# Turns of u and of the scores at the start of a fused attention and gated feed-forward kernel: their places in the transpose queue are given by a table

## The chip, the cores and the metric

One core of one Trainium2 chip. The metric is the device time of one execution in microseconds (us); less is better. The engines are called by the names of the profile: PE (TensorE, matrix products), DVE (VectorE), ACT (ScalarE), POOL (GpSimd) and SP (SyncE). SP computes nothing here: it issues all DMA transposes, one after another. POOL issues nearly all loads from memory, and ACT issues the stores.

## The reference

Eight sequences of 3008 tokens pass through a gated attention with squared-ReLU scores, and the result through a feed-forward layer with activation h cos(h):

```
scores = (z @ z.T) / S                  # z: 8 x 3008 x 64, S = 3008
attn   = max(scores, 0) ** 2
x      = u * (attn @ v)                 # u, v: 8 x 3008 x 256
h      = x @ w_in                       # w_in: 256 x 2048
out    = (h * cos(h)) @ w_out           # w_out: 2048 x 256
```

Since the same z stands on both sides, the matrix of scores is symmetric. Inputs and output are in float32; the kernel computes in float16 and accumulates in float32.

## The kernel before, in words

A sequence (the code calls it a batch, b = 0 to 7) is cut into six columns c of 512 tokens, and the scores into square tiles (c, R) of column and row, 512 by 512. The columns pass one after another. For each tile PE makes the scores (`s_matmuls`, L265), ACT or DVE takes the ReLU (L301, L299), and DVE squares it (L303) into one of 18 slots of SBUF, named `s`. PE then multiplies the tiles of a column with v into two banks of PSUM, `acc` (L353, or L466 for columns that use a scheme with seven products in place of eight, whose sums DVE prepares at L423, L425 and L435). At a column's end `finish` gates: DVE multiplies `acc` with the transposed u, named `ut`, into x (L382). That frees the two banks for the next column. The feed-forward layer follows 512 tokens at a time: `h_quantum` (PE L500, ACT L504, DVE L507) and `y_quantum` (PE L517), spread between the work of the attention.

Because of the symmetry a tile (c, R) with R > c serves column c as it is, and column R when it is transposed. The transpose is a DMA from slot to slot, issued by SP (L310). Columns 0 to 2 of the first batch are different: `direct` says that all six of their tiles are computed, so that they wait for no transpose. Their tiles with R = 3, 4 and 5 are turned all the same, since columns 3, 4 and 5 read them: nine transposes, called (0,3) to (2,5) in this text. Pairs (3,4), (3,5) and (4,5) follow, and from then on the kernel is in its steady course. Column 3 reads (0,3), (1,3) and (2,3), in the sums at L423.

Other transposes share SP's queue: `turn_u` (L181) makes `ut` of one column, called ut(0) to ut(5) here; `turn_z` (L144) and the tiles on the diagonal (L290) have theirs. `load_u`, `load_v`, `load_w_in` and `load_w_out` (all at L121) are issued by POOL. u is staged in two buffers `ust` in turn, so that u of column c + 2 is loaded after u of column c has been turned. `hold` lets a load or a turn of u or z wait for the PE product that was written down last before it, so that it isn't issued too early. A score transpose has no such hold: it waits for its data and its slot.

What sets the order: the kernel writes its steps into a list `events`, each with a time in units in which a column takes eight (U = 8) and a rank, sorts the list and calls the steps in that order. The framework then schedules what was recorded, engine by engine, by priority and by what is ready; `chain` holds PE to the written order, and `after(..., NOSYNC)` holds one instruction behind another without a wait on the chip. In this kernel a score transpose is recorded in `s_squares`, right behind the last square of its tile, and `turn_u` of the first batch stands at times 1, 5 and 10 for columns 0, 1 and 2:

```python
at(t + c * U + (1 if b or c not in (1, 2) else -3 * c), 0, lambda b=b, c=c: turn_u(b, c))
```

`use` notes from when to when each slot is needed, and `place` gives out the slots by it.

Of the kernel before, what the change touches and what calls it, by code (L numbers as in the profile page):

```python
# [14 lines left out]
def kernel(  # L15
# [9 lines left out]
    nc = tc.nc  # L25
# [21 lines left out]
    U = 8  # L47
# [186 lines left out]
    def direct(b, c, R):  # L234


        return b == 0 and c <= 2
# [5 lines left out]
    halves = {}  # L243
    slot_of = {}

    def slot(*key):
        return slots[slot_of[key]].rearrange("p (s k w) -> p s k w", s=K, w=P)

# [23 lines left out]
    def s_squares(b, c, R, p, banks):  # L272
        if p == 0:
            halves[(b, c, R)] = slot("a", b, c, R)
        t = halves[(b, c, R)]
        diagonal = triangle(b, c, R)
        rt = rpool.tile([P, 2, CW], FP16, name="rt")
        if diagonal:

            for i in range(2):  # L280
                k = 2 * p + i
                nc.scalar.activation(rt[:, i, k * P:], banks[k][:, k * P:], AF.Relu)  # L282
                sq = t[:, k, k:, :].rearrange("p s w -> p (s w)")
                if False:
                    nc.scalar.activation(sq, rt[:, i, k * P:], AF.Square)
                else:
                    nc.vector.tensor_tensor(
                        sq, rt[:, i, k * P:], rt[:, i, k * P:], ALU.mult)
                if k < K - 1:
                    nc.sync.dma_start_transpose(  # L290
                        t[:, k + 1:, k, :],
                        t[:, k, k + 1:, :].rearrange("p s w -> p (s w)"))
            if p == 1:
                fresh[(b, c, R)] = [t[:, k, :, :] for k in range(K)]
            return
        for i in range(2):
            k = 2 * p + i
            if direct(b, c, R) and (k == 3 or c == R == 0 and i):
                nc.vector.tensor_scalar_max(rt[:, i, :], banks[k], 0.0)  # L299
            else:  # L300
                nc.scalar.activation(rt[:, i, :], banks[k], AF.Relu)  # L301
        rv = rt.rearrange("p k (s w) -> p k s w", s=K)
        nc.vector.tensor_tensor(  # L303
            t.rearrange("p s k w -> p k s w")[:, 2 * p:2 * p + 2], rv, rv, ALU.mult)
        if p == 1:
            fresh[(b, c, R)] = [t[:, :, k, :] for k in range(K)]
            if R > c and not direct(b, R, c):
                tt = slot("t", b, c, R)
                turned[(b, c, R)] = tt
                nc.sync.dma_start_transpose(  # L310
                    tt.rearrange("p s k w -> p (s k) w"),
                    t.rearrange("p s k w -> p (s k w)"))

    def s_visit(pairs, also=None):
        done = [(pair, s_matmuls(*pair)) for pair in pairs]
# [51 lines left out]
    def finish(b, c):  # L367
        acc = accs[(b, c)]
        w = wide(b, c)
        t0 = b * S + c * CW  # L370
        ut = uts[(b, c)]
        o, parts = 0, []
        while o < w:
            m, at = (t0 + o) // TW, (t0 + o) % TW
            n = min(w - o, TW - at)
            if m not in xs:
                xs[m] = xpool.tile([P, NDH, TW], FP16, name="x")
            parts.append((xs[m][:, :, at:at + n], o, n))
            o += n
        for nh in range(NDH):  # L380
            for x, o, n in parts:
                nc.vector.tensor_tensor(  # L382
                    x[:, nh, :], acc[nh][:, o:o + n], ut[:, nh, o:o + n], ALU.mult)


    def v_sums(b, R):
# [126 lines left out]
    def y_quantum(m, ts, f4):  # L513
        if f4 == 0:
            ys[m] = ps_w.tile([P, CW], FP32, name="w")
        for ft in range(f4 * FG, (f4 + 1) * FG):
            chain(nc.tensor.matmul(  # L517
                ys[m][:, 0:D], gs[(m, f4)][:, ft % FG, ts * P:(ts + 1) * P],
                w_out16[:, ft, :], start=(ft == 0), stop=(ft == NFT - 1)))
        if f4 == NFT // FG - 1:  # L520
            if ts % 2 == 0:
                obs[m] = opool.tile([P, 2, D], FP32, name="ob")
            i = ts % 2
            nc.scalar.activation(  # L524
                obs[m][:, i, :], ys[m][:, 0:D], AF.Copy, bias=0.0, scale=inv_s2)
            i0 = i if m == NT - 1 else 0
            if i or m == NT - 1:
                r0 = m * TW + (ts - i + i0) * P
                nc.scalar.dma_start(
                    out[r0:r0 + (i + 1 - i0) * P, :].rearrange("(ts p) d -> p ts d", p=P),  # L530
                    obs[m][:, i0:i + 1, :])
# [4 lines left out]
    def at(t, rank, f):  # L536
        events.append((t, rank, len(events), f))
# [42 lines left out]
    for t, some in scores:  # L580
        for b, c, R, p in some:
            use(("a", b, c, R), t, t + 1)
            if p == 1 and R > c and not direct(b, R, c):
                use(("t", b, c, R), t + 0.8, t + 2.5)
                use(("a", b, c, R), t, t + 3)
    for b in range(B):
# [68 lines left out]
    for m in range(NT):  # L655
        b, i = divmod((m + 1) * TW - 1, S)
        th = max(20 + m * U, (b * NC + i // CW + 1) * U + 2)
        for ft in range(NFT):
            at(th + ft // 4 * 2 + ft % 4 * 0.2, 1, lambda m=m, ft=ft: h_quantum(m, ft))
        for ts in range(NTS):  # L660
            for f4 in range(NFT // FG):
                at(th + U + 2 * ts + 0.1 + 0.2 * f4, 4,
                   lambda m=m, ts=ts, f4=f4: y_quantum(m, ts, f4))
    for b in range(B):
        t = b * span
        if b == 0:
            for g in range(NG):
                at(-100 + g, 0, lambda g=g: first_z_load(g))
                at((-30, -2.5, 0.8)[g], 0, lambda g=g: first_z_turn(g))
            first = [lambda: load_v(0, 0), lambda: load_u(0, 0), lambda: load_v(0, 1),  # L670
                     lambda: load_v(0, 2), lambda: load_u(0, 1)]
            for i, f in enumerate(first):
                at(-80 + i, 0, f)
            at(-70, 0, gate.clear)
            at(2, 0, lambda: load_u(0, 2))
            for q in range(4):
                at(4 + 2 * q, 0, lambda q=q: load_w_in(q))
                at(17 + 2.5 * q, 0, lambda q=q: load_w_out(q))
        else:
            at(t - 3.5 * U, 0, lambda b=b: load_z(b))  # L680
            at(t - 2.5 * U, 0, lambda b=b: turn_z(b))
            for g in range(NG):
                at(t + (-1.5, -0.4, -0.1)[g] * U, 0, lambda b=b, g=g: load_v(b, g))
        for c in range(3 if b == 0 else 0, NC):
            at(t + (c - 1.25) * U, 0, lambda b=b, c=c: load_u(b, c))
        for c in range(NC):
            at(t + c * U + (1 if b or c not in (1, 2) else -3 * c), 0, lambda b=b, c=c: turn_u(b, c))

    def prepare():

# [48 lines left out]
```

## Time and profile before

| | |
|---|---|
| median of 8 runs | 1220.04 us (1217.81 to 1221.58) |
| profiled execution, its own time | 1220.7 us |
| span of the profiled execution | 1218.5 us |
| PE busy | 1207.3 us, 99% of the span |
| DVE busy | 1028.2 us, 84% |
| ACT busy | 833.3 us, 68% |
| POOL busy | 146.1 us, 12% |
| queue of SP's transposes and first loads (q1) | 88.73 MB, 44.5% of 16 engines |
| queue of POOL's loads (q0) | 29.77 MB, 24.5% |
| score transposes (s<-s, issued by SP) | 249, 4.3 us from issue to landing in the median |

A profile is of one execution. Busy shares are means over stages with different limits: here the first 80 us, in which the pipeline fills, differ from the rest. A line of a timeline gives the start in us, the length in us, the engine, the line of the code, the operation with output and input, the number of instructions that were merged, and in brackets the idle time of the engine before it with what ended that. For SP the length is that of issuing; the landing comes later. A line of the chain gives start, length and what the end waited for. A line of the windows gives the stretch and its length, then busy time with the number of instructions for PE, PE's weight load, DVE, ACT and POOL, then the granted clock of PE (1.00 is full), the busy share of the DMA engines (above 1 where packets overlap), and GB/s. Lines of a DMA queue give packets, MB and the time of its packets as a share of 16 engines.

### The profile page before, as it was taken

The page shows a single profiled execution, that of the slowest core. Times are in us where ns is not written, and L with a number is a line of the kernel's source. Part 1 is how long each engine was busy: PE and PEld are TensorE (multiplying, and loading weights), DVE is VectorE, ACT ScalarE, POOL GpSimd, SP SyncE. Part 2 cuts the span into 40 slices and gives each one's busy share as a digit, 9 for nine tenths or more (in the row PEclk, how much of TensorE's full clock was granted, in tenths as well). Part 3 has the DMA queues.
Part 4 walks back from the last instruction along what each step waited for, and adds up shares of the span by engine and source line. Part 5 has one row for each costly group of instructions (what it writes and reads, how often), then busy time and mean ns, then how long its engine had stood idle before and what let it go on. Part 6 is the DMA issues. An engine that isn't in the chain of part 4 may idle for free.

```text
span 1218.5 us, 23077 instructions
## 1 busy us (share of the span) xinstructions
PE 1207.3 (99%) x8439; PEld 769.2 (63%) x8439; DVE 1028.2 (84%) x2073; ACT 833.3 (68%) x1744; POOL 146.1 (12%) x201
## 2 busy tenths in 40 slices
PE   9899999999999999999999999999999999999998
PEld 3356666666666666666666666666666666666666
DVE  7888988889888898888988888888888888888875
ACT  6567766677666777667767677776777767767555
POOL 3210101001010010100101001010110111100000
PEclk9999999999999999999999999999999999999999
DMA  9997958779687895768967679585796857957311
GB/s 165 159 170 112 143 104 124 123 111 149 99 120 123 121 145 99 123 112 127 148 106 117 109 120 155 102 128 105 111 154 103 132 103 111 160 94 119 74 30 49
DMA packets 484226, 145.02 MB, mean 119 GB/s; under 512 B 432401, under 2 KB 484113, under 8 KB 484113
## 3 DMA queue, kind: packets, MB, share of 16 engines
q1 hardware_dynamic: 356448, 88.73, 44.5%
q0 software_dynamic: 100400, 29.77, 24.5%
q10 hardware_dynamic: 27264, 25.06, 6.4%
q8 instruction: 66, 1.08, 0.4%
q14 instruction: 48, 0.39, 0.1%
HBM read 60.29 MB, written 24.64 MB: 70 GB/s over the span
## 4 chain that ended last, share of the span: by engine, by line
PE 96%; DMA 2%; DVE 1%; ACT 0%; issue 0%; DVEq 0%; ACTq 0%
PE w L517 27%; PE w L500 26%; PE acc L466 19%; PE acc L353 17%; PE w L265 6%; DMA ut<-ust 1%; PE acc L330 1%; DMA s<-s 1%; DVE s L303 0%; PE w L696 0%; DVE g L507 0%; DVE x L382 0%; DVE s L435 0%; ACT rt L301 0%; DVE rt L299 0%
## 5 line engine op out<-in xcount | busy, mean ns | idle before, releaser
L504 ACT ACTIVATE c<-w 128x512 f16<-128x512 f32 x752 | 437.3, 619 | 259.2 <-PE w L500 206.4
L507 DVE TENSOR_TENSOR g<-w,c 128x512 f16<-128x512 f32 x752 | 492.2, 683 | 60.3 <-ACT c L504 57.4
L517 PE MATMUL w<-w_out,g 128*128 128x256 f16 x3008 | 448.7, 273 | 0.0
L500 PE MATMUL w<-x,w_in 128*128 128x512 f16 x1504 | 445.8, 379 | 0.0
L517 PEld LDWEIGHTS <-g 128*128 128x128 f16 x3008 | 294.4, 98 | 191.0
L353 PE MATMUL acc<-s,v 128*128 128x512 f16 (+1 forms) x1000 | 287.0, 379 | 3.3 <-DVE x L382 3.3
L301 ACT ACTIVATE rt<-w 128x512 f16<-128x512 f32 x489 | 253.1, 613 | 47.9 <-PE w L265 47.9
L303 DVE TENSOR_TENSOR s<-rt 128x1024 f16<-128x1024 f16 x254 | 172.7, 688 | 85.3 <-ACT rt L301 84.4
L500 PEld LDWEIGHTS <-w_in 128*128 128x128 f16 x1504 | 147.0, 98 | 73.8 <-issue 3.7
L466 PE MATMUL acc<-s,vsum 128*128 128x256 f16 (+1 forms) x1208 | 157.9, 270 | 0.9 <-DVE q L482 0.7
L121 POOL DMA_DIRECT2D ust<-in_u_dram x112 | 81.3, 731 | 571.4 <-PE acc L353 541.2
L353 PEld LDWEIGHTS <-v 128*128 128x128 f16 x1000 | 93.2, 98 | 78.0 <-issue 34.6
L466 PEld LDWEIGHTS <-vsum 128*128 128x128 f16 x1208 | 117.2, 98 | 20.0 <-issue 4.4
L466 PE MATMUL acc<-s,v 128*128 128x256 f16 (+1 forms) x906 | 117.6, 270 | 0.0
L466 PEld LDWEIGHTS <-v 128*128 128x128 f16 x906 | 85.4, 98 | 20.4 <-issue 12.4
L435 DVE TENSOR_TENSOR s<-s,s 128x1024 f16<-128x1024 f16 (+1 forms) x151 | 94.6, 668 | 2.7 <-PE acc L466 2.7
L265 PE MATMUL w<-zT 64*128 64x512 f16 (+3 forms) x684 | 91.6, 363 | 2.6 <-ACT zT L226 1.1
L524 ACT ACTIVATE ob<-w 128x256 f32<-128x256 f32 x188 | 71.1, 378 | 10.7 <-PE w L517 10.7
L382 DVE TENSOR_TENSOR x<-acc,ut 128x64 f16<-128x64 f32 (+7 forms) x178 | 68.6, 428 | 3.3 <-DMA ut<-ust 3.2
L282 ACT ACTIVATE rt<-w 128x512 f16<-128x512 f32 (+3 forms) x176 | 62.8, 449 | 10.5 <-PE w L265 10.5
L121 POOL DMA_DIRECT2D v<-in_v_dram x40 | 31.3, 788 | 298.1 <-PE acc L466 144.0
L425 DVE TENSOR_TENSOR s<-s 128x512 f16<-128x512 f16 (+1 forms) x151 | 61.2, 411 | 2.0
(37 smaller groups left out, 364.7 us busy)
## 6 DMA issues: line engine op xcount, KB each, us to landing
out_dram<-ob ACTq DMA_DIRECT2D x92, 256.0 KB, 2.2
ust<-in_u_dram POOLq DMA_DIRECT2D x80, 128.0 KB, 4.4
v<-in_v_dram POOLq DMA_DIRECT2D x16, 512.0 KB, 6.5
s<-s SPq DMA_TRANSPOSE x249, 4.3
v<-in_v_dram POOLq DMA_DIRECT2D x8, 448.0 KB, 9.4
zst<-in_z_dram POOLq DMA_DIRECT2D x14, 128.0 KB, 5.2
ust<-in_u_dram POOLq DMA_DIRECT2D x16, 96.0 KB, 5.0
w_in<-in_moe_w_in_dram POOLq DMA_DIRECT2D x4, 256.0 KB, 11.7
```

Source lines behind the costliest of these rows:

```text
L121: hold(nc.gpsimd.dma_start(dst, src))
L265: chain(nc.tensor.matmul(sp[:, s0 * P:], zt[h, R * K + k + 1 - lo, :], zt[h, j0 + s0:j0 + K, :].rearrange("p j w -> p (j w)"), start=True, ...
L301: nc.scalar.activation(rt[:, i, :], banks[k], AF.Relu)
L303: nc.vector.tensor_tensor(t.rearrange("p s k w -> p k s w")[:, 2 * p:2 * p + 2], rv, rv, ALU.mult)
L353: chain(nc.tensor.matmul(acc[:, 0:wn], vs(b, j // G)[:, j % G, nh * P:(nh + 1) * P], a, start=(start and n == 0), stop=(last and n == len( ...
L435: after(nc.vector.tensor_tensor(dst, src, sub, ALU.subtract).ins, before[-1], NOSYNC)
L466: chain(nc.tensor.matmul(acc[bank][:, cols], lhs[:, k, :], rhs[:, k, :] if old else rhs[:, :, k * P:(k + 1) * P], start=(n in (1, 5) and i ...
L500: chain(nc.tensor.matmul(hp, w_in16[:, k, ft * P:(ft + 1) * P], x[:, k, :], start=(k == 0), stop=(k == NDH - 1)))
L504: nc.scalar.activation(c16, hp, AF.Sin, bias=math.pi / 2.0, scale=inv_s2)
L507: nc.vector.tensor_tensor(gs[(m, ft // FG)][:, ft % FG, :], hp, c16, ALU.mult)
L517: chain(nc.tensor.matmul(ys[m][:, 0:D], gs[(m, f4)][:, ft % FG, ts * P:(ts + 1) * P], w_out16[:, ft, :], start=(ft == 0), stop=(ft == NFT ...
L524: nc.scalar.activation(obs[m][:, i, :], ys[m][:, 0:D], AF.Copy, bias=0.0, scale=inv_s2)
```

## The change

A table `TURNS` gives each score transpose of columns 0 to 2 of the first batch a time of its own. The step that turns a tile becomes a function, `turn_s`; for pairs in the table it is no longer called behind the tile's squares but put in the event list at the table's time with rank 3.5. Pairs with `None` are not turned, as before. `turn_u` of columns 0, 1 and 2 of the first batch moves from times 1, 5 and 10 to 0.7, 0.8 and 3.0. The times at which a slot is needed follow the table. Third, `finish` notes the last gating instruction of each of the columns 0 to 2, and `behind` orders later ReLUs and squares of these columns behind it on DVE, without a wait on the chip.

```diff
--- before.py
+++ after.py
@@ -243,6 +243,11 @@
     halves = {}
     slot_of = {}
 
+    TURNS = {(0, 0, 1): None, (0, 0, 2): None, (0, 1, 2): None,
+             (0, 0, 3): 1.0, (0, 0, 4): 2.4, (0, 1, 3): 7.8, (0, 0, 5): 8.0,
+             (0, 2, 3): 14.4, (0, 1, 4): 14.6, (0, 2, 4): 15.8, (0, 1, 5): 20.0,
+             (0, 2, 5): 22.0}
+
     def slot(*key):
         return slots[slot_of[key]].rearrange("p (s k w) -> p s k w", s=K, w=P)
 
@@ -296,20 +301,25 @@
         for i in range(2):
             k = 2 * p + i
             if direct(b, c, R) and (k == 3 or c == R == 0 and i):
-                nc.vector.tensor_scalar_max(rt[:, i, :], banks[k], 0.0)
+                behind(nc.vector.tensor_scalar_max(rt[:, i, :], banks[k], 0.0).ins)
             else:
                 nc.scalar.activation(rt[:, i, :], banks[k], AF.Relu)
         rv = rt.rearrange("p k (s w) -> p k s w", s=K)
-        nc.vector.tensor_tensor(
-            t.rearrange("p s k w -> p k s w")[:, 2 * p:2 * p + 2], rv, rv, ALU.mult)
+        ins = nc.vector.tensor_tensor(
+            t.rearrange("p s k w -> p k s w")[:, 2 * p:2 * p + 2], rv, rv, ALU.mult).ins
+        if direct(b, c, R):
+            behind(ins)
         if p == 1:
             fresh[(b, c, R)] = [t[:, :, k, :] for k in range(K)]
-            if R > c and not direct(b, R, c):
-                tt = slot("t", b, c, R)
-                turned[(b, c, R)] = tt
-                nc.sync.dma_start_transpose(
-                    tt.rearrange("p s k w -> p (s k) w"),
-                    t.rearrange("p s k w -> p (s k w)"))
+            if R > c and (b, c, R) not in TURNS:
+                turn_s(b, c, R)
+
+    def turn_s(b, c, R):
+        tt = slot("t", b, c, R)
+        turned[(b, c, R)] = tt
+        nc.sync.dma_start_transpose(
+            tt.rearrange("p s k w -> p (s k) w"),
+            halves[(b, c, R)].rearrange("p s k w -> p (s k w)"))
 
     def s_visit(pairs, also=None):
         done = [(pair, s_matmuls(*pair)) for pair in pairs]
@@ -379,8 +389,17 @@
             o += n
         for nh in range(NDH):
             for x, o, n in parts:
-                nc.vector.tensor_tensor(
-                    x[:, nh, :], acc[nh][:, o:o + n], ut[:, nh, o:o + n], ALU.mult)
+                ins = nc.vector.tensor_tensor(
+                    x[:, nh, :], acc[nh][:, o:o + n], ut[:, nh, o:o + n], ALU.mult).ins
+        if direct(b, c, c):
+            ended[:] = [ins]
+
+    ended = []
+
+    def behind(ins):
+
+        if ended:
+            after(ins, ended[0], NOSYNC)
 
 
     def v_sums(b, R):
@@ -580,7 +599,8 @@
     for t, some in scores:
         for b, c, R, p in some:
             use(("a", b, c, R), t, t + 1)
-            if p == 1 and R > c and not direct(b, R, c):
+            if p == 1 and R > c and TURNS.get((b, c, R), t) is not None:
+                t = TURNS.get((b, c, R), t)
                 use(("t", b, c, R), t + 0.8, t + 2.5)
                 use(("a", b, c, R), t, t + 3)
     for b in range(B):
@@ -661,6 +681,9 @@
             for f4 in range(NFT // FG):
                 at(th + U + 2 * ts + 0.1 + 0.2 * f4, 4,
                    lambda m=m, ts=ts, f4=f4: y_quantum(m, ts, f4))
+    for key, t in TURNS.items():
+        if t is not None:
+            at(t, 3.5, lambda key=key: turn_s(*key))
     for b in range(B):
         t = b * span
         if b == 0:
@@ -684,7 +707,7 @@
         for c in range(3 if b == 0 else 0, NC):
             at(t + (c - 1.25) * U, 0, lambda b=b, c=c: load_u(b, c))
         for c in range(NC):
-            at(t + c * U + (1 if b or c not in (1, 2) else -3 * c), 0, lambda b=b, c=c: turn_u(b, c))
+            at(t + c * U + (1 if b or c > 2 else (0.7, -7.2, -13.0)[c]), 0, lambda b=b, c=c: turn_u(b, c))
 
     def prepare():
```

## The prediction

> **What bounds the kernel now.** I read the windows by stage first, then the chain that ended last, then the timelines of SP, DVE and POOL in the first 80 us. From 75 us on TensorE (PE) is never idle:
>
> ```profile
> 75.00:1200.00 1125.00, 1125.00 (x7978) 731.16 (x7977) 958.20 (x1944) 776.72 (x1635) 124.07 (x167) 1.00 0.73 116
> ```
>
> So only the start can change the time: what PE is late by at 75 us, the end is late by. There the chain leaves the engines twice, for DMA transposes:
>
> ```profile
> 30.32 11.95 DMA ut<-ust
> 42.36 0.70 DVE x L382
> 43.11 1.90 PE acc L353 x6
> ...
> 52.27 10.09 DMA s<-s
> 62.38 0.42 DVE s L423
> ```
>
> The first is the turn of u for column 1, ut(1). It is issued at 30.32, lands at 42.27, and column 1's gating on VectorE (DVE, L382) waits 3.17 us for it. The second is the score transpose of pair (2,3), the last that column 3's sums (L423) read: issued at 52.27, landed at 62.35. DVE's own timeline has both waits:
>
> ```profile
> 42.36 1.29 DVE L382 TENSOR_TENSOR x<-acc,ut 128x512 f16<-128x512 f32 x2 [3.17 <-DMA ut<-ust]
> ...
> 62.38 0.42 DVE L423 TENSOR_TENSOR s<-s 128x512 f16<-128x512 f16 x1 [0.65 <-DMA s<-s]
> ```
>
> The second wait is only 0.65 us because DVE came late, by the first. Why both transposes are late is in SP's queue:
>
> ```profile
> 13.75 1.35 SPq L181 DMA_TRANSPOSE ut<-ust  x1
> 17.14 13.02 SPq L310 DMA_TRANSPOSE s<-s  x3
> 30.32 4.59 SPq L181 DMA_TRANSPOSE ut<-ust  x1
> 35.01 7.03 SPq L310 DMA_TRANSPOSE s<-s  x1
> 42.20 1.23 SPq L181 DMA_TRANSPOSE ut<-ust  x1
> 43.52 28.64 SPq L310 DMA_TRANSPOSE s<-s  x7
> 72.32 1.48 SPq L181 DMA_TRANSPOSE ut<-ust  x1
> ```
>
> From 17.14 to 73.8 us one issue follows the last within 0.2 us, and issues of equal size take from 2.1 to 7.0 us: SP is pushed back by transfers that are not drained. The page's DMA row is 9 in the first three slices. **This stage is bound by DMA, and the 3.17 us on DVE lie beside it, not in front of it.**
>
> **What the Trainium skill says.** "DMA: Bandwidth & Descriptors", section "Issuing engines are not separate DMA queues": transfers issued by SP, ACT and GpSimd run on the same 16 DMA engines and interleave. The trace agrees. Alone (41.4 to 44.4 us) the transposes' queue q1 moved 0.75 MB in 3 us; beside the loads issued by POOL (63 to 66 us) it moved 0.11 MB in the same time:
>
> ```profile
> q1 hardware_dynamic: 3004, 0.75, 122.5%
> ```
>
> ```profile
> q0 software_dynamic: 1269, 0.44, 124.6%
> q1 hardware_dynamic: 449, 0.11, 28.3%
> ```
>
> "TensorE: Matmul & The Clock Gate", Part 1, says that the matmul clock falls back after an idle stretch of some 3.4 us. It agrees: after the 3.34 us gap that PE shows ahead of 43.11 the granted clock was 0.65 for 4.9 us.
>
> ```profile
> 43.10:48.00 4.90, 4.89 (x16) 1.34 (x15) 4.52 (x10) 1.57 (x3) 1.96 (x3) 0.65 1.07 145
> 43.50:61.70 18.20, 17.98 (x81) 6.41 (x79) 17.79 (x39) 11.69 (x23) 8.45 (x12) 0.91 1.45 173
> 63.40:75.00 11.60, 10.41 (x65) 5.88 (x65) 11.54 (x24) 9.14 (x22) 0.75 (x1) 1.00 1.33 227
> ```
>
> **The change, part by part.**
>
> *No instruction is added or removed.* In the built program PE, DVE, ACT and POOL keep their order, instruction for instruction. The edges of `behind` cost nothing: in both builds the gating stands ahead of the next squares. Gain 0, loss 0; nothing has to cover it.
>
> *SP's order.* Before: ut(0), (0,3), (0,4), (0,5), ut(1), (1,3), ut(2), (1,4), (1,5), (2,3), (2,4), (2,5), (3,4), (3,5), ut(3). After: ut(0), ut(1), (0,3), (0,4), ut(2), (0,5), (1,3), (1,4), (1,5), (2,3), and the rest as before. So ut(1) passes three score transposes and ut(2) passes two. **The score transposes keep their order among themselves**: (1,4) and (1,5) still stand ahead of (2,3), though the table gives them later times. The times set a priority, and the program that comes out takes what is ready first.
>
> *ut(1).* It waits for the load of u for column 1, whose second half was issued at 10.60 and landed 8.2 us later, at 18.8. Issued then, with 1.3 us of issue and even the 12 us that it took before, it is there by 32. Column 1's gating wants it at 39.2. The 3.17 us on DVE and 3.34 us on PE go.
>
> *What that brings DVE to.* DVE is busy 17.79 of 18.20 us from 43.5 to 61.7, so all of it moves up by 3.2 us (by 3.6 if the 0.4 idle goes too). L423 on (2,3), reached at 61.73 before, is reached at about 58.5. It is next in line and DVE runs in order: queued behind it are a gated product (L507), L425, column 2's gating (L382) and the squares, all of which PE needs back to free its banks. PE stops there soon after DVE.
>
> *When (2,3) lands.* Ten transposes end by 62.35 before: three of u and seven of scores. The same ten stand up to (2,3) after. Corrections:
> - Start of the queue: (0,3) was issued at 17.14 and now follows ut(1), at about 20.2. The queue then ran at 257 GB/s (21 to 24 us); ut(0) still fills part of the gap. From 0 to 1 us lost, 0.6 taken.
> - ut(0) waits for the PE group that ends near 12.6 instead of the one that ends at 13.68: up to 1.1 us sooner, and the load behind it too. ut(2) must wait for that load (near 28.5), during which (0,4) still drains. Together from -1.1 to +1; -0.9 taken.
> - Loads. POOL waits for PE's progress and, for u of column 3, for ut(1):
>
> ```profile
> 42.83 1.49 POOL L121 DMA_DIRECT2D ust<-in_u_dram  x2 [12.73 <-DMA ut<-ust]
> ...
> 58.45 0.79 POOL L121 DMA_DIRECT2D w_out<-in_moe_w_out_dram  x1 [2.21 <-PE acc L353]
> 59.23 1.51 POOL L121 DMA_DIRECT2D ust<-in_u_dram  x2
> ```
>
> With PE 3.2 us ahead these three go out at about 55.2 to 57.5, before DVE and PE stop, and so run in front of the end of (2,3); before, they ran behind it (63 to 66 us). They cost the transposes 0.75 - 0.11 = 0.64 MB at 0.25 MB/us, 2.6 us. All of it if (2,3) is still wholly open, none if it ends first: 0 to 2.6; 2.6 taken, since loads and transposes ahead of it are the same work as before.
>
> Sum: 62.35 + 0.6 - 0.9 + 2.6 = 64.65, **2.3 us later than before**, with ends from -1.1 to +4.6. DVE then waits about 6 us instead of 0.65.
>
> *The clock.* PE's stop moves to about 59 to 65 and is longer. The slow stretch cost 4.89 x (1 - 0.65) = 1.7 us before, beside a full DVE. After, it falls into 64 to 70, where PE has 11.60 - 10.41 = 1.2 us of idle time to hide it: 0.5 comes through (0 to 1.7).
>
> *New buffers.* The slots are placed anew. New waits on a transpose: a square of (3,4) for (1,4), due near 55.7 when (1,4), landed at 52.4 before, should be there by 55; the diagonal of column 4 for (1,5); column 4's scratch for (2,5), landed at 70.3 and wanted at 76.3. (3,4) waits on SP for (2,4) ahead of it. Bounds 0 to 1 us, 0 taken: the slack of several us covers them, and DVE stands at (2,3) behind them.
>
> Total: +2.3 + 0.5 = **+2.8 us**. The profiled execution took 1220.7 (span 1218.5 and 2.2 around it), 0.7 above the median of 1220.04. On its own time that is 1223.5; on the median, 1222.8.
>
> **Rivals.**
>
> *A, the forecast (0.50): the stall moves to (2,3) and grows.* For it: an unbroken queue and unchanged order of scores. 1222.8; alone 1221 to 1226.
>
> *B (0.21): (2,3) lands when it did.* The same ten transfers, the loads falling beside them without net loss. DVE continues at 62.4 as before: 1220.0. Nothing in the trace shows an idle DMA that would make it better; what speaks for it is that the 2.6 and the 0.6 are my largest free terms.
>
> *C (0.29), the other side: the queue was held back by its order.* If the mix of loads and transposes moves to better places, u of column 3 filling 38 to 42 where DMA now trails, and (2,3) lands by 58.5, DVE never stops: the whole 3.17 + 0.65 + 0.4 = 4.2 us is gained, 1215.9. It decides from a landing before 62.35 on, microsecond for microsecond. For it: q1 fell to 134 GB/s in all with the loads from 27 to 36, so the sharing is inefficient and can change. Against it: 3.8 us are 0.95 MB at full rate, nearly the two transposes (1,4) and (1,5) that have not moved behind.
>
> **How the numbers follow.** This kernel's time can be told from no change at about 0.2%, 2.4 us. A lies mostly above that, B inside it, C mostly below. Faster 0.28, same 0.20, slower 0.52. The range runs from C's full gain with a little more, 1215.4, to A with most of its upper ends, 1225.8.
>
> **What would show it.** Right: ut(1) issued near 19 and no DVE wait at L382; then a DVE wait of 4 to 8 us at L423 on s<-s ending after 63 us; the chain with one long DMA s<-s and no DMA ut<-ust in the first 60 us; PE's gap near 59 to 65 with a clock below 0.8 after it; w_out and u loads issued near 55 to 57. Wrong: L423's wait ending before 61 us, or SP's queue with gaps, or PE idle anywhere after 75 us, which my sum has none of.

## The result and the profile after

The kernel after takes **1229.22 us** in the median of 11 runs (1222.47 to 1233.74). The kernel before, timed beside it, takes 1219.36 (32 runs, 1217.29 to 1223.71). The ratio is 1.0079, with a 95% interval of 1.0066 to 1.0093: slower by 9.9 us. Here and below the ratio follows the means of the runs, so it can differ from that of the two medians. The sign of the forecast was right. The size was not: 2.8 us were forecast, and the result lies above the upper end of the range, 1225.8.

The profiled execution took 1231.64 us. Its page begins:

```profile
span 1229.5 us, 23076 instructions
...
PE 1207.8 (98%) x8439; PEld 769.4 (63%) x8439; DVE 1027.8 (84%) x2073; ACT 833.5 (68%) x1744; POOL 146.0 (12%) x201
```

The span is 11.0 us longer than before, and PE is busy 0.5 us longer. So nearly all of the loss, 10.5 us, is PE standing idle. The windows say where (columns as before). From 100 us on PE is never idle; the hole is at 57 to 70, followed by a slow clock, and 0.6 us of idle time are left between 75 and 90:

```profile
50.00:60.00 10.00, 6.74 (x30) 2.66 (x30) 3.08 (x6) 5.01 (x10) 2.86 (x5) 0.99 1.58 144
60.00:70.00 10.00, 0.48 (x1) 0.10 (x1) 3.52 (x8) 0.44 (x1) 0.00 (x0) 0.50 1.43 204
70.00:80.00 10.00, 8.01 (x36) 3.66 (x35) 7.45 (x15) 6.53 (x14) 0.74 (x1) 0.66 1.05 186
...
100.00:1210.00 1110.00, 1110.00 (x7880) 722.18 (x7879) 946.41 (x1918) 767.39 (x1615) 121.43 (x163) 1.00 0.73 117
```

DVE's timeline of the kernel after shows what it waits for. The lines of the code have moved: the gating L382 is now L392, the sums L423 and L425 are L442 and L444, the squares L303 are L308, the score transposes L310 are L320, `s_matmuls` L265 is L270, and g (L507) is L526.

```profile
38.31 1.28 DVE L392 TENSOR_TENSOR x<-acc,ut 128x512 f16<-128x512 f32 x2
...
63.12 0.43 DVE L444 TENSOR_TENSOR s<-s 128x512 f16<-128x512 f16 x1 [10.04 <-DMA s<-s]
...
64.06 0.42 DVE L442 TENSOR_TENSOR s<-s 128x512 f16<-128x512 f16 x1
...
67.84 0.69 DVE L308 TENSOR_TENSOR s<-rt 128x1024 f16<-128x1024 f16 x1 [3.36 <-DMA s<-s]
...
72.04 0.43 DVE L442 TENSOR_TENSOR s<-s 128x512 f16<-128x512 f16 x1 [1.38 <-DMA s<-s]
```

Column 1's gating, which waited 3.17 us for ut(1) and started at 42.36, now starts at 38.31 without a wait. In its place there are three waits on score transposes. The first, 10.04 us, ends with (1,3), which landed at 63.0: L444 writes column 3's scratch, and `place` has put that into the slot that the turn of (1,3) still reads. (The next sum, L442 at 64.06, reads (1,3) itself.) The second, 3.36 us, is for the slot that the turn of (1,4) reads. Only the third, 1.38 us, is for the tile (2,3), which landed at 72.0. Before, (2,3) landed at 62.35, so it is 9.7 us later; but DVE had lost most of its time before it came to it. PE stops behind DVE, as its timeline shows:

```profile
69.52 1.78 PE L270 MATMUL w<-zT 64*128 64x512 f16 x3 [11.92 <-DVE g L526]
73.12 0.58 PE L270 MATMUL w<-zT 64*128 64x512 f16 x1 [1.82 <-DVE g L526]
```

These two gaps are 13.7 us; the gap of 3.34 us that PE had ahead of 43.11 is gone. The difference, 10.4 us, is nearly the whole loss. The chain that ended last tells the same: no DMA of `ut` in it, one long stretch of score transposes.

```profile
52.49 4.83 SPq L320
57.40 14.62 DMA s<-s x2
72.47 0.61 DVE g L526
```

SP's queue shows why the score transposes are late:

```profile
11.88 9.91 SPq L181 DMA_TRANSPOSE ut<-ust  x2
21.89 17.40 SPq L320 DMA_TRANSPOSE s<-s  x2
39.46 3.67 SPq L181 DMA_TRANSPOSE ut<-ust  x1
43.21 39.03 SPq L320 DMA_TRANSPOSE s<-s  x9
82.41 1.23 SPq L181 DMA_TRANSPOSE ut<-ust  x1
```

Two turns of u stand at the head and hold SP for 9.9 us. The second waits for the load of u for column 1, whose last half was issued by POOL at 10.38 and landed at 20.5. Only then is ut(1) issued, and the first score transpose follows at 21.89 instead of 17.14. The view of the DMA queues shows what that stretch carried. From 20.5 to 25 us, before:

```profile
q1 hardware_dynamic: 3616, 0.92, 99.7%
q0 software_dynamic: 65, 0.02, 3.8%
```

and after:

```profile
q0 software_dynamic: 903, 0.23, 51.9%
q1 hardware_dynamic: 1075, 0.27, 35.7%
```

Before, this stretch was nearly free of loads, and the transposes (q1) had it for themselves: 0.92 MB. Now they move 0.27 MB in it. By the time that they are queued, the loads of u for column 2 and of w_in (q0), which POOL issued from 20.87 on, are there too. I call this **the lost window**. The rest of the stage, in MB read from the same view:

| stretch, us | q1 before | q1 after | q0 before | q0 after |
|---|---|---|---|---|
| 20.5 to 25 | 0.92 | 0.27 | 0.02 | 0.23 |
| 25 to 36 | 0.38 | 0.50 | 1.09 | 0.78 |
| 36 to 44.4 | 1.13 | 0.51 | 0.21 | 0.37 |
| 44.4 to 53 | 0.74 | 0.60 | 0.52 | 0.68 |
| 53 to 62.3 | 1.14 | 0.74 | 0.66 | 0.62 |
| sum | 4.31 | 2.62 | 2.50 | 2.68 |

By 62.3 us the transposes are 1.69 MB behind, while the loads are only 0.18 MB ahead. The two kinds together move less. Besides the lost window the largest loss is in 36 to 44.4, where before the transposes had a second quiet time. POOL's timeline shows what is in it now: u of column 3 is loaded from 35.93 on, and w_out follows sooner, because PE is ahead and ut(1) no longer holds the load back.

```profile
35.93 1.49 POOL L121 DMA_DIRECT2D ust<-in_u_dram  x2 [6.63 <-PE acc L363]
41.37 0.74 POOL L121 DMA_DIRECT2D w_out<-in_moe_w_out_dram  x1 [3.95 <-PE w L270]
```

Before, the same loads were issued at 42.83 and 46.31. I call this **the loads on the transposes**.

### The profile page after: what moved, and what is told of

Same layout as the page of the kernel before. It is cut to its first block, busy times and chain, and to the rows that moved or that the text cites. A ratio compares the mean times of both kernels' runs of the same rounds, so it can differ in the third digit from the quotient of the medians.

```text
span 1229.5 us, 23076 instructions
## 1 busy us (share of the span) xinstructions
PE 1207.8 (98%) x8439; PEld 769.4 (63%) x8439; DVE 1027.8 (84%) x2073; ACT 833.5 (68%) x1744; POOL 146.0 (12%) x201
## 4 chain that ended last, share of the span: by engine, by line
PE 96%; DVE 2%; DMA 1%; ACT 1%; issue 0%; SPq 0%; ACTq 0%; DVEq 0%
PE w L536 27%; PE w L519 26%; PE acc L485 19%; PE acc L363 17%; PE w L270 6%; DMA s<-s 1%; PE acc L340 1%; DVE s L308 1%; SPq L320 0%; DVE g L526 0%; PE w L719 0%; ACT rt L306 0%; DVE rt L304 0%; ACT zT L226 0%; DVE s L454 0%
## 5 line engine op out<-in xcount | busy, mean ns | idle before, releaser
L526 DVE TENSOR_TENSOR g<-w,c 128x512 f16<-128x512 f32 x752 | 492.3, 683 | 61.8 <-ACT c L523 58.9
L308 DVE TENSOR_TENSOR s<-rt 128x1024 f16<-128x1024 f16 x254 | 172.6, 687 | 88.0 <-ACT rt L306 83.8
L270 PE MATMUL w<-zT 64*128 64x512 f16 (+3 forms) x684 | 92.3, 360 | 16.9 <-DVE g L526 14.7
L485 PEld LDWEIGHTS <-v 128*128 128x128 f16 x906 | 85.5, 98 | 20.6 <-issue 12.9
L444 DVE TENSOR_TENSOR s<-s 128x512 f16<-128x512 f16 (+1 forms) x151 | 61.2, 411 | 11.9 <-DMA s<-s 10.0
L287 ACT ACTIVATE rt<-w 128x512 f16<-128x512 f32 (+3 forms) x176 | 62.8, 449 | 10.5 <-PE w L270 10.5
L392 DVE TENSOR_TENSOR x<-acc,ut 128x64 f16<-128x64 f32 (+7 forms) x178 | 68.5, 428 | 0.1
L270 PEld LDWEIGHTS <-zT 64*128 64x128 f16 x684 | 25.6, 94 | 66.8 <-issue 53.1
```

Of the source, the lines that this page charges most:

```text
L270: chain(nc.tensor.matmul(sp[:, s0 * P:], zt[h, R * K + k + 1 - lo, :], zt[h, j0 + s0:j0 + K, :].rearrange("p j w -> p (j w)"), start=True, ...
L308: ins = nc.vector.tensor_tensor(t.rearrange("p s k w -> p k s w")[:, 2 * p:2 * p + 2], rv, rv, ALU.mult).ins
L485: chain(nc.tensor.matmul(acc[bank][:, cols], lhs[:, k, :], rhs[:, k, :] if old else rhs[:, :, k * P:(k + 1) * P], start=(n in (1, 5) and i ...
L526: nc.vector.tensor_tensor(gs[(m, ft // FG)][:, ft % FG, :], hp, c16, ALU.mult)
```

## The experiments

The theories. *Turns:* the whole loss is in the turns of u, through the lost window, through the loads on the transposes, or both. *Table:* it is in the new places of the score transposes, the slots that follow them, or the edges of `behind`. In some of the runs the executions of one kernel fall into a shorter and a longer group; a profile shows one execution, so the text says which.

**1. Only the turns of u, in the kernel before** (label e1_u_turns).

```diff
-            at(t + c * U + (1 if b or c not in (1, 2) else -3 * c), 0, lambda b=b, c=c: turn_u(b, c))
+            at(t + c * U + (1 if b or c > 2 else (0.7, -7.2, -13.0)[c]), 0, lambda b=b, c=c: turn_u(b, c))
```

> The kernel before, with the new times of the three turns of u alone: no table, the old slots. SP's order becomes that of the changed kernel: ut(0), ut(1), (0,3), (0,4), ut(2), (0,5), (1,3). Theory W (window): with ut(1) second, SP stands before a load that lands at 20.5 us, and the stretch from 20.5 to 25 us, in which no loads run, passes nearly unused (0.27 MB of transposes instead of 0.92): all of the loss is here, 1227 to 1231 us. Theory L (lead): PE without its stop brings the later loads forward onto the transposes; also 1227 to 1231. Theory S (slots): the loss comes from the new waits on slots that the table brings (DVE's 10.0 us at the scratch of column 3 and 3.4 us at the square of (3,4)); then no more than my forecast is left here, 1220 to 1223.

Measured: 1228.26 us (20 runs), ratio 1.0057 (1.0044 to 1.0070). The queue has the same head, the window is lost in the same way, and of the waits DVE's on score transposes (L303, in the numbering of before; total, times and longest in us) is the large one. Its longer part is for a slot too: the turn of (1,3) reads until 59.8 what a tile of column 2 is to be written over. (2,3) landed at 66.7, 3 us before DVE came to it. The profile, at 1228.85, is of the longer group: fifteen of the runs lie from 1227.5 to 1229.9, five from 1220.5 to 1224.7. The lines are of SP's queue, of the DMA queues from 20.5 to 25, and of the waits:

```profile
12.21 9.86 SPq L181 DMA_TRANSPOSE ut<-ust  x2
```

```profile
q1 hardware_dynamic: 1056, 0.26, 36.9%
```

```profile
DVE s L303 <- DMA s<-s: 11.3, 2, 9.1
```

**2. All but the turns of u** (label e2_table): the kernel after with the turns where they were.

```diff
-            at(t + c * U + (1 if b or c > 2 else (0.7, -7.2, -13.0)[c]), 0, lambda b=b, c=c: turn_u(b, c))
+            at(t + c * U + (1 if b or c not in (1, 2) else -3 * c), 0, lambda b=b, c=c: turn_u(b, c))
```

> The changed kernel with the old times of the turns of u: table, new slots and the order edges on DVE stay. SP's order is that of the kernel before. W and L: as the kernel before, 1219.4 within 2 us, with DVE's 3.2 us wait for ut(1) back. S: most of the loss remains, above 1225.

Measured: 1219.72 us (20 runs), ratio 0.9994 (0.9984 to 1.0003). By themselves the table, the slots and the edges cost nothing that can be measured. With run 1 this puts the loss into the turns of u, 7.0 of 9.9 us by the ratios. The two intervals just meet (1.0070 and 1.0066), so these two runs don't exclude that the table adds the rest, some 3 us, once the turns are early; run 12 bears on that.

**3. The table's order enforced** (label e3_forced). In the kernel after the score transposes keep their old order in spite of the table. Here each is held behind the one ahead of it in the table, so that (2,3) stands ahead of (1,4) and (1,5).

```diff
+    queued = []
...
+        if (b, c, R) in TURNS:
+            if queued:
+                after(ins, queued.pop(), NOSYNC)
+            queued.append(ins)
```

> The changed kernel with the score transposes of the table held to the table's order on SP: (1,3), (0,5), (2,3), (1,4), (2,4), (1,5), (2,5). Pair (2,3) passes (1,4) and (1,5). W and L: the transfers are as late as in the changed kernel, but the wait for (2,3) is shorter by up to two transposes, while the square of (3,4) still waits for (1,4) on its slot, now behind (2,3): 2 to 4 us better than the changed kernel, 1225 to 1227. If the order of the scores were the whole cause: 1216 or below. If it plays no part: 1229.

Measured: 1228.04 us (20 runs, 1220.35 to 1233.21), ratio 1.0058 (1.0042 to 1.0074). By the ratios this is 2.6 us better than the kernel after, at the edge of what the two intervals allow. In the profile (2,3) landed at 63.5, only 1.2 us later than before. Yet DVE waits 9.4 us, in the squares of (3,4), for the slot that the turn of (1,4) reads until 65.3; the wait at the sums is 1.6 us:

```profile
DVE s L308 <- DMA s<-s: 9.4, 1, 9.4
```

So the order among the score transposes is worth little: the queue as a whole is late, and now (1,4), put behind (2,3), holds DVE by its slot.

**4. ut(1) early, but behind two score transposes** (label e5_ut1_third). In the kernel before, ut(1) is placed between (0,4) and (0,5). The window should stay, and the wait at the gating should go.

```diff
+        if (b, c) == (0, 1):
+            after(turn.ins, queued.pop(), NOSYNC)
+            queued.append(turn.ins)
...
+                if (b, c, R) == (0, 0, 4):
+                    queued.append(ins)
+                if (b, c, R) == (0, 0, 5):
+                    after(ins, queued.pop(), NOSYNC)
...
+            at(t + c * U + (1 if b or c > 2 else (1, -5.5, -6.0)[c]), 0, lambda b=b, c=c: turn_u(b, c))
```

> The kernel before, with ut(1) held behind (0,4) and ahead of (0,5) on SP, nothing else. It uses the stretch without loads (two score transposes pass from 17 to 24 us as before) and ut(1) is there by about 30, so DVE's 3.2 us wait at the gating of column 1 goes. W alone: nothing is lost, 1215 to 1219. L: PE leads by 3.2 us, the loads of u for columns 3 and 4, w_out and z come forward onto the transposes as in the changed kernel, and (2,3) lands later than 62.4: 1221 to 1224.

Measured: 1224.94 us (20 runs), ratio 1.0020 (1.0000 to 1.0040). The window is whole, and the gating doesn't wait. But waits on score transposes remain, at the squares (L308 in this kernel) and at the sums (L432). The lines are of the DMA queues from 20.5 to 25 and of the waits:

```profile
q1 hardware_dynamic: 3618, 0.92, 99.6%
```

```profile
DVE s L308 <- DMA s<-s: 4.3, 1, 4.3
DVE s L432 <- DMA s<-s: 1.9, 1, 1.9
```

The lost window is thus not all of it: with the window kept, PE's lead alone still makes the kernel no faster in the mean. The runs lie in two groups, eight from 1215.3 to 1218.5 and eleven from 1224.1 to 1230.3, with one at 1221.0. A median between two groups says little of a mechanism. The profile is of the longer group; (2,3) landed at 63.5 in it.

**5. The window mended in the kernel after** (label e8_after_u1_first): u of column 1 is loaded ahead of the second and third part of v, so that ut(1) needn't wait.

```diff
-            first = [lambda: load_v(0, 0), lambda: load_u(0, 0), lambda: load_v(0, 1),
-                     lambda: load_v(0, 2), lambda: load_u(0, 1)]
+            first = [lambda: load_v(0, 0), lambda: load_u(0, 0), lambda: load_u(0, 1),
+                     lambda: load_v(0, 1), lambda: load_v(0, 2)]
```

> The changed kernel with u of column 1 loaded ahead of v's second and third parts instead of behind them: ut(1) can go out right behind ut(0), near 14 us, and SP no longer stands before a load until 20.5. W: the window from 20.5 to 25 us is used (0.7 to 0.9 MB of transposes in place of 0.27), and the time falls by W's share to that of the kernel with ut(1) third, 1223 to 1226, plus up to 1 us for v arriving later at PE. If the window doesn't matter: 1228 to 1231.

Measured: 1222.87 us (20 runs, 1216.89 to 1228.11), ratio 1.0015 (0.9996 to 1.0034). SP is held for 5.24 us instead of 9.91, and 0.25 of the 0.65 MB lost in the window are back; by 36 us the transposes have moved 1.36 MB from 20.5 on, against 0.77 in the kernel after and 1.30 before. A wait at the sums of 6.8 us remains, and one of 1.4 us at the squares. Nine of the runs lie from 1216.9 to 1219.5 and ten from 1224.3 to 1228.1; the profile, at 1226.24, is of the longer. The same order of loads was not tried in the kernel before. SP's queue, the DMA queue from 20.5 to 25, and the waits:

```profile
11.80 5.24 SPq L181 DMA_TRANSPOSE ut<-ust  x2
```

```profile
q1 hardware_dynamic: 2057, 0.52, 86.2%
```

```profile
DVE s L442 <- DMA s<-s: 6.8, 1, 6.8
```

**6. Loads late, with ut(1) third** (label e6_third_late): run 4, and w_out, z of the next batch and u of columns 3 and 4 are loaded later.

```diff
-                at(17 + 2.5 * q, 0, lambda q=q: load_w_out(q))
+                at(22.5 + 1.2 * q, 0, lambda q=q: load_w_out(q))
...
-            at(t - 3.5 * U, 0, lambda b=b: load_z(b))
+            at(t - 3.5 * U + (4 if b == 1 else 0), 0, lambda b=b: load_z(b))
...
-            at(t + (c - 1.25) * U, 0, lambda b=b, c=c: load_u(b, c))
+            at(t + (c - 1.25) * U + ({3: 8, 4: 4}.get(c, 0) if b == 0 else 0), 0, lambda b=b, c=c: load_u(b, c))
```

> The kernel with ut(1) behind (0,4), and besides the loads that meet the transposes from 36 to 62 us held to later PE products: u of columns 3 and 4 (8 and 4 time units later), w_out (from 22.5 on, 1.2 apart) and z of the next batch (4 units later). Theory L (lead): what that kernel lost were loads that came forward with PE onto the transposes; now (1,4), (1,5) and (2,3) land before DVE asks for them (56 to 58.5 us) and both waits are gone: 1213 to 1217, faster than both kernels. If the loss came from another source, a wait on slots or the transposes' own speed: 1222 to 1226 as without the later loads.

Measured: 1223.03 us (20 runs), ratio 1.0028 (1.0018 to 1.0037). The total lies where the other source was expected, not theory L. But no wait on a score transpose is left: (2,3) lands at 50.7, and PE starts a group at 69.14 us that it started at 74.71 before, 5.6 us ahead. Then it loses this lead, because w_out now comes too late. The waits show it (L526 is the product of `y_quantum` in this kernel):

```profile
PE w L526 <- DMA w_out<-in_moe_w_out_dram: 5.1, 2, 4.6
```

**7. Loads late, in the kernel after** (label e7_after_late).

```diff
+                at(22.5 + 1.2 * q, 0, lambda q=q: load_w_out(q))
...
+            at(t - 3.5 * U + (4 if b == 1 else 0), 0, lambda b=b: load_z(b))
...
+            at(t + (c - 1.25) * U + ({3: 8, 4: 4}.get(c, 0) if b == 0 else 0), 0, lambda b=b, c=c: load_u(b, c))
```

> The changed kernel with the same loads held later. W (window) by itself: 0.65 MB of transposes are still missing at 25 us, 2.6 us at full rate; without L they land 2 to 4 us later than in the same kernel with ut(1) third. If L is the larger part of the 9.7 us, the queue catches up alone at 0.25 MB/us and (2,3) lands by 60: 1214 to 1220. If the lost window is the larger part: 1223 to 1228.

Measured: 1226.70 us (6 runs), ratio 1.0057 (1.0040 to 1.0075). The window is lost as in the kernel after (q1 moves 0.27 MB in it), yet q1 then moves 1.36 MB from 36 to 44.4 where the kernel after moves 0.51, (2,3) lands at 55.6 instead of 72.0, and no wait on `s` is left. PE waits 7.7 us for w_out instead, which is why the total again misses the range that the landing would give.

**8. The control: loads late, in the kernel before** (label e9_before_late). The three added lines are the same:

```diff
+                at(22.5 + 1.2 * q, 0, lambda q=q: load_w_out(q))
...
+            at(t - 3.5 * U + (4 if b == 1 else 0), 0, lambda b=b: load_z(b))
...
+            at(t + (c - 1.25) * U + ({3: 8, 4: 4}.get(c, 0) if b == 0 else 0), 0, lambda b=b, c=c: load_u(b, c))
```

> The kernel before with the same loads held later: the control for them. DVE's 3.2 us wait for ut(1) stays, since what stands ahead of it, w_in and three score transposes, is untouched; the 0.65 us wait for (2,3) goes: 1218 to 1220. If later loads were a gain by themselves, without ut(1) moved: below 1217. If they starve a later step (column 3's u, the first products with w_out): above 1222.

Measured: 1225.46 us (12 runs), ratio 1.0050 (1.0035 to 1.0065), with a wait of 5.4 us for w_out. My late times were too late in themselves, so the totals of runs 6 and 7 price my times and not the theory; only the landings in them count.

**9. Middle times, with ut(1) third** (label e10_third_mid): run 4 with the loads moved less.

```diff
-                at(17 + 2.5 * q, 0, lambda q=q: load_w_out(q))
+                at(20.6 + 0.6 * q, 0, lambda q=q: load_w_out(q))
...
-            at(t - 3.5 * U, 0, lambda b=b: load_z(b))
+            at(t - 3.5 * U + (3.5 if b == 1 else 0), 0, lambda b=b: load_z(b))
...
-            at(t + (c - 1.25) * U, 0, lambda b=b, c=c: load_u(b, c))
+            at(t + (c - 1.25) * U + ({3: 5.5, 4: 2.5}.get(c, 0) if b == 0 else 0), 0, lambda b=b, c=c: load_u(b, c))
```

> ut(1) behind (0,4), as before, and the loads held less than in the last three: u of column 3 later by 5.5 units and of column 4 by 2.5, z of the next batch by 3.5, and w_out at 20.6 to 22.4 instead of 17 to 24.5, so that its four parts come ahead of z and of u of column 4. Theory L: in the kernel with all loads late no DVE wait for a score transpose was left, and PE stood 5.7 us ahead of the kernel before at 69 us, until it waited 5.1 us for w_out. With w_out in time that lead stays: 1213 to 1216. If the transposes are pushed out again: DVE waits on s<-s return and it is 1219 to 1223.

Measured: **1215.86 us** (9 runs), ratio 0.9968 (0.9954 to 0.9983), faster than both kernels. No wait on `s`, `ut` or w_out is left, and (2,3) lands at 55.7. In the windows DVE is busy without a pause from 43 to 62.3 and PE from 75 to 90, at a full clock:

```profile
43.00:62.30 19.30, 18.27 (x97) 8.06 (x96) 19.30 (x41) 14.68 (x31) 7.91 (x11) 1.00 1.33 196
75.00:90.00 15.00, 15.00 (x111) 10.14 (x109) 11.55 (x24) 8.72 (x19) 2.37 (x4) 1.00 0.77 140
```

**10. Its control: middle times, in the kernel before** (label e11_before_mid).

```diff
+                at(20.6 + 0.6 * q, 0, lambda q=q: load_w_out(q))
...
+            at(t - 3.5 * U + (3.5 if b == 1 else 0), 0, lambda b=b: load_z(b))
...
+            at(t + (c - 1.25) * U + ({3: 5.5, 4: 2.5}.get(c, 0) if b == 0 else 0), 0, lambda b=b, c=c: load_u(b, c))
```

> The kernel before with the same middle times of the loads, the control. No wait for w_out; the 3.2 us wait for ut(1) stays. If the gain needs both, the lead and the free DMA: 1217.5 to 1219.5. If the times of the loads alone make it: below 1216.5.

Measured: 1218.50 us (20 runs), ratio 0.9987 (0.9979 to 0.9994). The middle times alone bring 1.6 us; the gating still waits 2.9 us for ut(1).

**11. Middle times, in the kernel after** (label e12_after_mid).

```diff
+                at(20.6 + 0.6 * q, 0, lambda q=q: load_w_out(q))
...
+            at(t - 3.5 * U + (3.5 if b == 1 else 0), 0, lambda b=b: load_z(b))
...
+            at(t + (c - 1.25) * U + ({3: 5.5, 4: 2.5}.get(c, 0) if b == 0 else 0), 0, lambda b=b, c=c: load_u(b, c))
```

> The changed kernel with the same middle times of the loads. With the late loads its (2,3) landed at 55.6 us in spite of the lost window, ahead of DVE's need at 58.5, and PE then waited 7.7 us for w_out. If the loads on the transposes are what the changed kernel pays for, and the lost window only adds to it: 1213 to 1219, faster than the kernel before. If the window by itself is enough to lose: 1222 to 1226.

Measured: 1224.06 us (20 runs), ratio 1.0016 (0.9998 to 1.0033). Eight of the runs lie between 1216.07 and 1218.92, twelve between 1222.66 and 1228.45. The profile is of one of the eight: (2,3) lands at 59.8 and DVE waits 2.8 us for it. The window is lost there too, and q1 moves 1.48 MB from 36 to 44.4. So moving these loads alone doesn't mend it reliably.

**12. Both parts mended in the kernel after** (label e13_both): the edit of run 5 and that of run 11.

```diff
+            first = [lambda: load_v(0, 0), lambda: load_u(0, 0), lambda: load_u(0, 1),
+                     lambda: load_v(0, 1), lambda: load_v(0, 2)]
...
+                at(20.6 + 0.6 * q, 0, lambda q=q: load_w_out(q))
...
+            at(t - 3.5 * U + (3.5 if b == 1 else 0), 0, lambda b=b: load_z(b))
...
+            at(t + (c - 1.25) * U + ({3: 5.5, 4: 2.5}.get(c, 0) if b == 0 else 0), 0, lambda b=b, c=c: load_u(b, c))
```

> The kernel after with both suspected parts mended: u of column 1 is loaded ahead of the second and third part of v (ut(1) is then issued early, and 20.5 to 25 us is used by transposes), and the loads of w_out, z and u of columns 3 and 4 stand at the middle times (they no longer fall on the transposes). Theory (lost window plus loads on the transposes, together all of the loss): sum (2,3) has its transpose by about 58 us, no wait for s<-s above 2 us, 1215 to 1218.5 us. Rival (something else in the change, such as ut(2) early or the slots, costs as well): 1221 us or more, with a wait for s<-s or another PE idle of 4 us or more after 50 us. If the late u loads alone set the time: no different from the kernel with the middle times and the old order of loads, a median near 1224.

Measured: **1216.20 us** (10 runs, 1215.80 to 1217.53), ratio 0.9975 (0.9966 to 0.9985). No wait on `s` or `ut` is left on DVE in the first 95 us, and (2,3) lands at 56.6. SP's queue and the windows:

```profile
12.68 5.18 SPq L181 DMA_TRANSPOSE ut<-ust  x2
17.97 7.24 SPq L320 DMA_TRANSPOSE s<-s  x2
25.57 2.05 SPq L181 DMA_TRANSPOSE ut<-ust  x1
27.71 45.58 SPq L320 DMA_TRANSPOSE s<-s  x9
```

```profile
43.00:62.00 19.00, 17.97 (x92) 7.25 (x91) 19.00 (x41) 14.02 (x29) 6.90 (x9) 1.00 1.40 187
75.00:1200.00 1125.00, 1125.00 (x7981) 731.29 (x7980) 957.54 (x1939) 776.57 (x1634) 123.94 (x167) 1.00 0.73 117
```

The first score transpose is issued at 17.97, near the 17.14 of before. From 20.5 to 62.3 us q1 moves 4.44 MB (0.48, 0.87, 1.05, 1.37 and 0.67 in the stretches of the table), against 2.62 in the kernel after and 4.31 before. The queue's order with the turns of u ahead, the table and its slots are the same as after. So none of these is a loss in itself. The loss came from ut(1) standing at the head before its load had landed, and from the loads that came forward.

**The sizes.** With the window mended the ratio falls from 1.0079 to 1.0015, with the loads moved to 1.0016, with both to 0.9975. At 1220 us that is 7.8 and 7.7 us each alone and 12.7 together; of the 7.7, 1.6 are there in the kernel before as well (run 10). Runs 5 and 11 are means over a shorter and a longer group, and the four intervals together leave some 4 us on the difference between 7.8 + 7.7 and 12.7. So the runs show that each part counts and that both together leave nothing of the loss, but not how the 9.9 us divide. What also stays open is why the executions with a partly mended queue fall into two groups.

## Why the prediction went wrong, step by step

*Only the start can change the time:* right. PE is never idle from 100 us on in the kernel after. "PE idle anywhere after 75 us, which my sum has none of" did happen, 0.6 us between 75 and 90, because the stage ends later.

*No cost of the instructions' order and of `behind`:* right, by run 2.

*"New buffers ... Bounds 0 to 1 us, 0 taken":* right only while the queue is on time (run 2). Of the 14.8 us that DVE waited, 13.4 were for slots that late transposes still read, ahead of its wait for (2,3) and not behind it. The prediction had the square of (3,4) in its list, but not column 3's scratch, which waits for (1,3). The slots themselves are not the cause: run 1, with the old ones, has such waits too, and the profiles of runs 7, 11 and 12, with the new ones, have none.

*Score transposes keep their order:* right. Run 3, where they don't, gains 2.6 us by the ratios, hardly clear of its uncertainty.

*ut(1) is there by 32 and the 3.17 and 3.34 us go:* right. ut(1) was issued at 20.6 and landed at 24.9, and the gating doesn't wait.

*The stage is bound by DMA, so the stall moves to the score transposes and grows* (rival A): right in kind. The place was wrong: DVE stopped first at L444 for the slot of (1,3), which stands three places ahead of (2,3) in the queue, and waited 14.8 us in three pieces, not 6. Had (2,3) alone been on time, DVE would have saved only the last 1.38 us (an estimate from its timeline); run 3, with (2,3) at 63.5, agrees.

*The sum for (2,3), +2.3 us; measured +9.7.* This is the step that failed: it made the queue, of which (2,3) is the tenth transpose, 2.3 us late where it was 9.7 us late. DVE pays for that lateness at the slots and tiles one after another, not at (2,3) alone. The terms of the sum are:

- **"Start of the queue ... From 0 to 1 us lost, 0.6 taken."** I counted the 3.1 us by which the first score transpose moves and let ut(0) fill part of it. It moved by 4.75 us (17.14 to 21.89), since the load of u(1) landed at 20.5 and not at 18.8. Above all, I took the time after it for as good as the time before it. It isn't: 20.5 to 25 was the part without loads. There 0.92 - 0.27 = 0.65 MB were lost, 2.6 us at my rate of 0.25 MB/us. The trace of before showed the 0.92 MB.
- "-0.9" for ut(0) and ut(2): ut(0) was issued 1.9 us sooner, more than the 1.1 that I allowed, and landed 0.9 us sooner. ut(2), issued only at 39.46 behind a (0,4) that took 19.1 us to land, brought nothing.
- **"Loads ... 0 to 2.6; 2.6 taken."** I moved three loads. All the loads behind PE's progress moved, and u of column 3 most, 6.9 us. I had shown its line, with the wait for ut(1) in it, and used it for ut(1) alone. In 36 to 44.4 the transposes lost 1.13 - 0.51 = 0.62 MB, 2.5 us; from 44.4 to 62.3, 0.54 MB, 2.2 us; in 25 to 36 they got back 0.12 MB, 0.5 us. What was lost after the window is thus 4.2 us where 2.6 were taken. That the loads have to do with it is shown by moving them (1.36 MB from 36 to 44.4 in run 7, 1.48 in run 11). But it isn't their bytes alone: in run 4, whose window is whole, u of column 3 and the first part of w_out were issued within 0.7 us of the same times and moved the same 0.37 MB there, and the transposes moved 1.10. So part of the 4.2 seems to need the lost window as well, and the two terms can't be kept apart. The three loads that I did price were issued at 53.69, 54.47 and 56.24, close to the 55.2 to 57.5 forecast.

With the 2.6 of the first these are 6.8 us of the 9.7; the other 2.9 are not accounted for at this rate. It is 0.25 MB/us, a rate of transposes alone; at 204 GB/s, which 60 to 70 us shows in all, the 1.69 MB are 8.3 us. (The 134 GB/s from 27 to 36 that I gave to q1 in rival C were of both queues; q1 alone moved 0.38 MB in these 9 us, 42 GB/s.) The error in kind was to hold transposes and loads for one amount of work ("loads and transposes ahead of it are the same work as before"): from 43 to 62 the two together moved 175 GB/s before and 145 after.

*The clock, +0.5:* not tested. PE's busy time did grow by 0.5 us in all, but that is not the time that comes through to the end, and the slow stretch fell later than the forecast 64 to 70. An estimate from the windows: the slow matmuls from 70 to 80 cost 8.01 x (1 - 0.66) = 2.7 us, 1.0 more than the 1.7 of before. That the number agrees is luck as far as is shown. "TensorE: Matmul & The Clock Gate" of the Trainium skill, Part 1, has the clock at half after an idle stretch; the window from 60 to 70 shows 0.50.

*Rival C* ("the queue was held back by its order", gain 4.2 us) has its mechanism in runs 9 and 12, not in this change: with the loads kept off the transposes the kernel is 3.1 to 3.9 us faster than before (0.9975 and 0.9968 of 1220). The shorter groups of runs 4, 5 and 11, from 1215.3 to 1219.5, are at or near it. Of the 3.1 to 3.9, 1.6 us are the loads' own (run 10), so the early turns of u bring 1.5 to 2.3 of the 3.17 us that the gating waited.

## What to carry to other kernels

A wait that lies beside a resource that is full can be removed without gain; then ask what the work that is now ahead will trigger, since loads gated by its progress come sooner and can fall on the transfers that bind. In an in-order queue put nothing at the head that waits for a load: what can be lost is not only the waiting time but the quiet stretch behind it, and a view of the queues in that very stretch, in MB, shows what is at stake. A transpose that is late also holds the slot that it reads, so list who writes that slot next, and don't look for the wait only where its result is read. Move the load with the step that reads it, and the later loads with the work that they would collide with.

## What was not expected of the hardware

Transfers of the two kinds did not share like one amount of bytes: from 43 to 62 us both queues together moved 175 GB/s before, 145 after and 187 in run 12. "DMA: Bandwidth & Descriptors" of the Trainium skill, section "Queues, rings and completion order", has each DMA engine change between queues packet by packet. The counts of packets here can't test that: from 53 to 62.3 us q0 had 3502 and q1 2948 after, 3682 and 4528 before. What it leaves unexplained is how long q1's own packets took from 41.4 to 44.4, by the queues' view of the kernel after:

```profile
q1 hardware_dynamic: 952, 0.24, 117.0%
q0 software_dynamic: 243, 0.06, 20.1%
```

Before, 3004 packets of q1 took 122.5% of the 16 engines in these 3 us, 20 ns each. Now 952 take 117.0%, 59 ns each, with only 0.06 MB of loads beside them. Over 36 to 44.4 a packet of q1 took 33 ns before (4515 packets, 109.4%) and 67 ns after (2039, 101.2%); it took 40 ns in run 1, 48 in run 5, 30 in run 4, 31 in run 11, 27 in run 7 and 35 in run 12. So they were longest where the window was lost and the loads came early, but run 1, which has both, is well below the kernel after. What made them three times as long is not settled.
